# Order edges in a linear attention with a gated feed-forward block: conversions behind kv, gate products behind an x product, projections behind all products

## The chip, the cores and the metric

The kernel runs on one core of one Trainium2 chip. The time of an execution is device microseconds from its start to its end; a profiled execution also has a span, from its first to its last instruction. Times of before are the median of three runs.

## What is computed

Eight batches of 576 tokens pass a linear attention with eight heads of 64, and all 4608 tokens then a gated feed-forward block of width 1536. Everything is float32.

```
q_s = softmax over d of q;  k_s = softmax over s of k
kv  = einsum('bhsd,bhse->bhde', k_s, v)
x   = einsum('bhsd,bhde->bhse', q_s, kv)   # heads side by side: 4608 x 512
out = ((x @ w_a) * (x @ w_b)) @ w_out      # 512 -> 1536 -> 512
```

The host lays the arrays out and passes the weights as raw 64-bit integers; the kernel turns them into float32 itself.

## The kernel before

**Tiles and stages.** Heads go in four pairs g (`NP`), so that one pair fills 128 partitions. Tokens go in nine chunks c of 512 (`NCH`), hidden features in twelve blocks f of 128 (`NF`), taken two at a time (i) from the second chunk on. Products of the attention's result with the weights take each float32 operand as a rounded part and a remainder (`split`, L76: a copy on ACT or DVE, a subtraction on DVE), and sum three matmuls.

**The start (L587 to L623).** For each pair of the first batch the exponential of k is made and transposed (`kv_soft_t`), q's softmax is made, `kv_product` multiplies k with v (PSUM tile pk, den, kv) and `kv_split` makes kvh and kvl, both on DVE. `q_transpose` gives pq and its parts qh (ACT) and ql (DVE); `x_product` multiplies them with kvh and kvl into px, three matmuls, and ACT and DVE split px into an operand tile xo. Behind the second pair stands `convert_f(0)`, behind the fourth `convert_f(1)`.

**Conversions.** `convert_f(f)` turns three raw tiles of block f into weights: two of the gate (`convert_ab`) and one of w_out (`convert_wo`). Each goes through `to_float` (L87): two ACT steps (L99, L100), a DVE shift (L102, raw<-wy), a POOL addition (L103, wr), a DVE merge (L104, wy). `convert_ab` then issues a store of wy on SP (dy), splits it (ACT copy and DVE subtraction, ws) and, for three of four tiles, stores the parts (dw); `convert_wo` stores wy into the w_out tile (wo_w<-wy, L128). The raw tiles share a ring of 11 buffers (tag xo) with the operand tiles of x.

**The first chunk (L633 to L648).** For each f: raw loads of a later block, `convert_f(f + 2)`, one call of `attend()` (the next chunk's attention, a list of ten entries: entry 0 holds the k and v loads of one pair alone, later entries a load, a softmax and a product of different pairs), `gate_first(f)` (24 matmuls into pt, n = 0 and 1; ga copied by ACT at L433 and multiplied by DVE at L434), and `project_first` of the block before (L458, po). At f = 11 the operands of the second chunk are made (`x_operands`), which need the x products of all four pairs (px of c = 1).

**Later chunks (L660 to L725).** Each pair of blocks takes seven products (`product`, L449, 12 matmuls each) in place of eight, with sums between them on DVE (u2, u3, cc) and a split of each gated block (gh on ACT, gl on DVE); `project` (L463) adds a block's 12 matmuls to four output tiles po. The projections of the pair before go between the products, but those of blocks 8 and 9, and of 10 and 11, of the last chunk are left for L724. `store` copies po out of PSUM, in the last chunk by halves (L477 on ACT, L478 on DVE), and issues the store on SP.

**What sets the order.** The framework plans each engine's instruction order ahead, by its own timeline and the order of the program: an instruction ready earlier in the plan goes ahead of one that stands earlier in the program but is ready later. On the chip each engine takes its instructions in the planned order. All DMAs are issued on one queue, SP. `tc.issue_after(ins)` adds an edge from `ins` to each instruction that the block makes on the engine of `ins`, and to no other.

## Time and profile before

| | us |
|---|---|
| median of three runs (lowest, highest) | 990.01 (989.1, 992.04) |
| profiled execution | 986.57 |
| its span | 984.5 |
| PE busy in the span | 948.7 (96%) |
| DVE, ACT, POOL busy | 632.5, 391.7, 112.8 |
| mean granted clock of PE | 0.99 of full speed |

PE is TensorE's matmuls and PEld its weight loads, DVE is VectorE, ACT ScalarE, POOL GpSimd; SPq is the queue that issues the DMAs. A matmul's row gives the time to its modelled end, and matmuls overlap, so that the sum of a group can pass the time to the next row. In a row of the timeline the square brackets tell how long the engine stood before it, and what released it.

### The profile page before, as it was taken

The page shows a single profiled execution, that of the slowest core. Times are in us where ns is not written, and L with a number is a line of the kernel's source. Part 1 is how long each engine was busy: PE and PEld are TensorE (multiplying, and loading weights), DVE is VectorE, ACT ScalarE, POOL GpSimd, SP SyncE. Part 2 cuts the span into 40 slices and gives each one's busy share as a digit, 9 for nine tenths or more (in the row PEclk, how much of TensorE's full clock was granted, in tenths as well). Part 3 has the DMA queues.
Part 4 walks back from the last instruction along what each step waited for, and adds up shares of the span by engine and source line. Part 5 has one row for each costly group of instructions (what it writes and reads, how often), then busy time and mean ns, then how long its engine had stood idle before and what let it go on. Part 6 is the DMA issues. An engine that isn't in the chain of part 4 may idle for free.

```text
span 984.5 us, 16997 instructions
## 1 busy us (share of the span) xinstructions
PE 948.7 (96%) x6171; PEld 854.0 (87%) x6171; DVE 632.5 (64%) x1259; ACT 391.7 (40%) x1087; POOL 112.8 (11%) x96
## 2 busy tenths in 40 slices
PE   3889999999999999999999999999999999999998
PEld 3757666899999999999999999999999999899996
DVE  7797786988686665656566657565656545653443
ACT  8666675542372325322442335223532263221111
POOL 3245344531000000000000000000000000000000
PEclk9799999999999999999999999999999999999999
DMA  9699858999989967997699779977998679767761
GB/s 346 228 412 397 340 207 293 358 332 303 307 279 338 321 241 280 334 334 259 240 339 328 267 258 341 320 264 252 337 295 295 232 282 288 269 230 262 256 212 46
DMA packets 93682, 283.64 MB, mean 288 GB/s; under 512 B 10848, under 2 KB 11424, under 8 KB 93600
## 3 DMA queue, kind: packets, MB, share of 16 engines
q1 hardware_dynamic: 93600, 282.57, 81.9%
q8 instruction: 49, 0.80, 0.3%
q14 instruction: 33, 0.27, 0.1%
HBM read 241.40 MB, written 37.98 MB: 284 GB/s over the span
## 4 chain that ended last, share of the span: by engine, by line
PE 70%; DMA 6%; DVE 2%; ACT 1%; issue 1%; SPq 0%; DVEq 0%
PE po L468 24%; PE kp L449 12%; PE ka L449 12%; PE kx L449 12%; PE ky L449 6%; DMA mr<-dq 4%; DMA qtt<-in_q_late 2%; PE pk L251 2%; PE px L381 2%; DMA dq<-sst 1%; DVE ws L82 0%; ACT qt L323 0%; SPq L347 0%; DVE ql L82 0%; ACT gh L79 0%
## 5 line engine op out<-in xcount | busy, mean ns | idle before, releaser
L468 PE MATMUL po<-wo_w,gh 128*128 128x512 f32 x768 | 226.5, 394 | 1.0 <-ACT gh L79 1.0
L449 PE MATMUL kx<-xo,ws 128*128 128x256 f32 x1152 | 164.8, 284 | 0.0
L449 PE MATMUL ka<-xo,ws 128*128 128x256 f32 x1152 | 163.1, 285 | 0.9 <-DVE cc L720 0.7
L468 PEld LDWEIGHTS po<-wo_w,gh 128*128 128x128 f32 x768 | 138.8, 189 | 27.3 <-ACT gh L79 1.4
L449 PE MATMUL kp<-xo,ws 128*128 128x256 f32 x1152 | 158.3, 284 | 1.1 <-DVE u L693 1.0
L449 PEld LDWEIGHTS ka<-xo,ws 128*128 128x128 f32 x1152 | 152.1, 192 | 4.5 <-DVE cc L720 0.9
L449 PEld LDWEIGHTS kx<-xo,ws 128*128 128x128 f32 x1152 | 151.9, 191 | 3.5 <-issue 0.5
L449 PEld LDWEIGHTS kp<-xo,ws 128*128 128x128 f32 x1152 | 148.2, 191 | 3.9 <-DVE u L693 1.2
L468 PE MATMUL po<-wo_w,gl 128*128 128x512 f32 x384 | 136.9, 395 | 0.0
L79 ACT CAST gh<-cc 128x512 fp32r<-128x512 f32 x96 | 57.6, 620 | 147.4 <-DVE cc L717 144.1
L716 DVE TENSOR_TENSOR cc<-kp,u 128x512 f32<-128x512 f32 x48 | 33.0, 688 | 89.1 <-PE kp L449 88.8
L323 ACT ACTIVATE qt<-qt,st 128x64 f32<-128x64 f32 x224 | 75.0, 336 | 34.7 <-DVE st L320 30.5
L468 PEld LDWEIGHTS po<-wo_w,gl 128*128 128x128 f32 x384 | 71.2, 188 | 15.3
L449 PE MATMUL ky<-xo,ws 128*128 128x256 f32 x576 | 78.5, 285 | 2.5 <-ACT xo L79 2.1
L426 PE MATMUL pt<-xo,ws 128*128 128x512 f32 x288 | 76.1, 415 | 3.0 <-ACT ga L433 3.0
L449 PEld LDWEIGHTS ky<-xo,ws 128*128 128x128 f32 x576 | 72.9, 192 | 3.2 <-ACT xo L79 2.4
L82 DVE TENSOR_TENSOR gl<-cc,gh 128x512 fp32r<-128x512 f32 x96 | 66.9, 704 | 9.6 <-ACT gh L79 9.4
L426 PEld LDWEIGHTS pt<-xo,ws 128*128 128x128 f32 x288 | 55.0, 194 | 19.3 <-ACT ga L433 4.0
L707 ACT COPY cc<-kx 128x256 f32<-128x256 f32 x48 | 17.7, 370 | 130.8 <-PE kx L449 122.1
L706 DVE TENSOR_TENSOR cc<-kp,u 128x512 f32<-128x512 f32 x48 | 32.9, 685 | 54.8 <-PE kp L449 54.8
L219 POOL PARTITION_ALL_REDUCE mx<-m x20 | 14.1, 704 | 467.2 <-DVE m L205 435.4
L355 ACT ACTIVATE qtt<-qtt 128x512 f32<-128x512 f32 x28 | 17.7, 633 | 103.9 <-DVE qtt L354 77.4
(127 smaller groups left out, 1241.8 us busy)
## 6 DMA issues: line engine op xcount, KB each, us to landing
ws<-dw SPq DMA_DIRECT2D x312, 512.0 KB, 5.2
dw<-ws SPq DMA_DIRECT2D x42, 512.0 KB, 5.0
mr<-dq SPq DMA_DIRECT2D x56, 256.0 KB, 6.5
raw<-in_w_ab SPq DMA_DIRECT2D x24, 512.0 KB, 7.9
out<-ot SPq DMA_DIRECT2D x36, 256.0 KB, 4.8
vt<-in_v SPq DMA_DIRECT2D x28, 325.0 KB, 7.3
qt<-in_q SPq DMA_DIRECT2D x32, 256.0 KB, 5.2
kt<-in_k SPq DMA_DIRECT2D x24, 320.0 KB, 5.8
```

Source lines behind the costliest of these rows:

```text
L79: nc.scalar.copy(out=hi, in_=src)
L82: nc.vector.tensor_tensor(out=lo, in0=src, in1=hi.bitcast(F32), op=ALU.subtract)
L251: nc.tensor.matmul(pk, kt[:, j].rearrange("p h d -> p (h d)"), vt[:, j], start=(j == 0), stop=(j == J - 1),)
L323: nc.scalar.activation(out=qt[:, j, h], in_=qt[:, j, h], func=AF.Exp, bias=st[:, h, 0, j:j + 1], accum_out=st[:, h, 1, j:j + 1],)
L355: nc.scalar.activation(out=qt, in_=qt, func=AF.Exp)
L381: nc.tensor.matmul(px[:, s], w, m[:, s], start=(i == 0), stop=(i == 2))
L426: nc.tensor.matmul(pt, w[:, wp], x[g][:, xp], start=(i == 0), stop=(i == 3 * NP - 1))
L449: nc.tensor.matmul(pt[:, n], w[:, n, wp, c], x[:, xp, c], start=(first and n == 0 and i == 0), stop=(i == 5), skip_group_check=True,)
L468: nc.tensor.matmul(po[t], a[:, ts], wo[f][:, w], start=(f == 0 and i == 0), stop=(f == NF - 1 and i == 2),)
L706: nc.vector.tensor_tensor(out=cc[:, 3], in0=kp, in1=u3, op=ALU.add)
L707: nc.scalar.copy(out=cc[:, 0, 0], in_=kx[:, 0])
L716: nc.vector.tensor_tensor(out=cc[:, 1], in0=kp, in1=u2, op=ALU.add)
```

## The change

The products and sums stay as they are. Edges of order are added at four places. The conversions of block 1 are made behind the kv subtractions of pairs 2 and 3; the first call of `attend` stands behind that of pair 3; the gate products of the first chunk's last block stand behind the second chunk's x product of pair 2; the projections that are left at the end stand behind the last product, and those of the last two blocks go one output tile after the other. The last chunk's output tiles are copied whole, the even ones on DVE, the odd ones on ACT.

```diff
@@ -76,10 +76,20 @@
     def split(hi, lo, src, hi_engine="act"):
 
         if hi_engine == "act":
-            nc.scalar.copy(out=hi, in_=src)
+            a = nc.scalar.copy(out=hi, in_=src)
         else:
-            nc.vector.tensor_copy(out=hi, in_=src)
-        nc.vector.tensor_tensor(out=lo, in0=src, in1=hi.bitcast(F32), op=ALU.subtract)
+            a = nc.vector.tensor_copy(out=hi, in_=src)
+        return a, nc.vector.tensor_tensor(out=lo, in0=src, in1=hi.bitcast(F32), op=ALU.subtract)
+
+    @contextmanager
+    def behind(point):
+
+        with ExitStack() as pinned:
+            for ins in marks.get(point, ()):
+                pinned.enter_context(tc.issue_after(ins.ins))
+            yield
+
+    marks = {}
 
 
     wo = {}
@@ -267,7 +277,7 @@
     def kv_split(b, g, kv):
         kvh = sb.tile([P, P], F32R, name=f"kvh{g}")
         kvl = sb.tile([P, P], F32R, name=f"kvl{g}")
-        split(kvh, kvl, kv, "dve")
+        marks["kv", b, g] = split(kvh, kvl, kv, "dve")[1:]
         kvs[b, g] = (kvh, kvl)
 
 
@@ -366,7 +376,7 @@
             )
         qh = sb.tile([P, T], F32R, name="qh", bufs=1)
         ql = sb.tile([P, T], F32R, name="ql", bufs=1)
-        split(qh, ql, pq)
+        marks["q"] = split(qh, ql, pq)
         return qh, ql
 
     def x_product(c, g, qhl, tag="at"):
@@ -378,7 +388,8 @@
         for b, s in ((b0, slice(0, n0)), (b1, slice(n0, T)))[:b1 - b0 + 1]:
             kvh, kvl = kvs[b, g]
             for i, (w, m) in enumerate(((kvh, qh), (kvh, ql), (kvl, qh))):
-                nc.tensor.matmul(px[:, s], w, m[:, s], start=(i == 0), stop=(i == 2))
+                ins = nc.tensor.matmul(px[:, s], w, m[:, s], start=(i == 0), stop=(i == 2))
+        marks["px", c, g] = (ins,)
         return px
 
 
@@ -446,12 +457,13 @@
             i = 0
             for c in range(2):
                 for wp, xp in ((0, 0), (0, 1), (1, 0)):
-                    nc.tensor.matmul(
+                    ins = nc.tensor.matmul(
                         pt[:, n], w[:, n, wp, c], x[:, xp, c],
                         start=(first and n == 0 and i == 0), stop=(i == 5),
                         skip_group_check=True,
                     )
                     i += 1
+        return ins
 
     def project_first(f, g, po):
         for t in range(TT):
@@ -460,22 +472,24 @@
                 start=(f == 0), stop=(f == NF - 1),
             )
 
-    def project(f, ghl, po):
+    def project(f, ghl, po, one_by_one=False):
         gh, gl = ghl
-        for t in range(TT):
-            ts = slice(t * P, (t + 1) * P)
-            for i, (a, w) in enumerate(((gh, 0), (gh, 1), (gl, 0))):
-                nc.tensor.matmul(
-                    po[t], a[:, ts], wo[f][:, w],
-                    start=(f == 0 and i == 0), stop=(f == NF - 1 and i == 2),
-                )
+        with ExitStack() as in_turn:
+            for t in range(TT):
+                ts = slice(t * P, (t + 1) * P)
+                for i, (a, w) in enumerate(((gh, 0), (gh, 1), (gl, 0))):
+                    ins = nc.tensor.matmul(
+                        po[t], a[:, ts], wo[f][:, w],
+                        start=(f == 0 and i == 0), stop=(f == NF - 1 and i == 2),
+                    )
+                if one_by_one:
+                    in_turn.enter_context(tc.issue_after(ins.ins))
 
     def store(c, po):
         for t in range(TT):
             ot = sb.tile([P, DM], F32, name="ot", tag="wr", bufs=4)
-            if c == NCH - 1:
-                nc.scalar.copy(out=ot[:, 0:H], in_=po[t][:, 0:H])
-                nc.vector.tensor_copy(out=ot[:, H:], in_=po[t][:, H:])
+            if c == NCH - 1 and t % 2 == 0:
+                nc.vector.tensor_copy(out=ot, in_=po[t])
             else:
                 nc.scalar.copy(out=ot, in_=po[t])
             nc.sync.dma_start(out=out[c * T + t * P:c * T + (t + 1) * P, :], in_=ot)
@@ -615,12 +629,20 @@
             q_soft_first(qt)
         kv_split(0, g, kv_product(kt, vt, ("po0", "po1")[odd]))
         qhl = q_transpose(qt, ("at", "k1")[odd])
+        marks["q", g] = marks["q"]
         px = x_product(0, g, qhl, ("po2", "po3")[odd])
         x = xo_tile([P, 2, T])
-        split(x[:, 0], x[:, 1], px)
+        marks["x", g] = split(x[:, 0], x[:, 1], px)
         x0.append(x)
-        if odd:
-            convert_f(g // 2)
+        if g == 1:
+            convert_ab(0, 0)
+            convert_ab(0, 1)
+            convert_wo(0)
+    with behind(("kv", 0, 2)):
+        convert_ab(1, 0)
+        convert_ab(1, 1)
+    with behind(("kv", 0, 3)):
+        convert_wo(1)
 
 
     early = (B11, T2, T3, T1)
@@ -636,14 +658,20 @@
                 last_load = load_f(n)
         if f + 2 < NF:
             convert_f(f + 2)
-        if f:
+        if f == 1:
+            with behind(("kv", 0, 3)):
+                attend()
+        elif f:
             attend()
         if f == NF - 1:
             sy[0] = sums(0)
             x_operands(xfs[1], early + late, xo)
-        ghl = gate_first(f, x0)
+        last_f = f == NF - 1
+        with behind(("px", 1, 2) if last_f else None):
+            ghl = gate_first(f, x0)
         if pending is not None:
-            project_first(*pending, po)
+            with behind(("px", 1, None) if last_f else None):
+                project_first(*pending, po)
         pending = (f, ghl)
     pend = [(pending[0], pending[1], 0, po)]
 
@@ -652,7 +680,10 @@
         if not pend:
             return
         f, ghl, c, po = pend.pop(0)
-        (project if c else project_first)(f, ghl, po)
+        if c:
+            project(f, ghl, po, c == NCH - 1 and f >= NF - 2)
+        else:
+            project_first(f, ghl, po)
         if f == NF - 1:
             store(c, po)
 
@@ -716,13 +747,14 @@
             nc.vector.tensor_tensor(out=cc[:, 1], in0=kp, in1=u2, op=ALU.add)
             nc.vector.tensor_tensor(out=cc[:, 1, 0], in0=cc[:, 1, 0], in1=cc[:, 1, 1], op=ALU.mult)
             g1 = g_split(2 * i, cc[:, 0:2, 0])
-            product(ka, operand(A22), x[T4], False)
+            last_product = product(ka, operand(A22), x[T4], False)
             nc.vector.tensor_tensor(out=cc[:, 2], in0=ka, in1=u2, op=ALU.add)
             last = nc.vector.tensor_tensor(out=cc[:, 2, 0], in0=cc[:, 2, 0], in1=cc[:, 2, 1], op=ALU.mult)
             g2 = g_split(2 * i + 1, cc[:, 2:4, 0])
             pend += [(2 * i, g1, c, po), (2 * i + 1, g2, c, po)]
-    while pend:
-        run_pending()
+    with tc.issue_after(last_product.ins):
+        while pend:
+            run_pending()
 
 
 def kernel(**inputs):
```

## Rows read from the trace of the kernel before

**Rows 1.** The page's engines: busy us, share of the span, instructions.

```profile
PE 948.7 (96%) x6171; PEld 854.0 (87%) x6171; DVE 632.5 (64%) x1259; ACT 391.7 (40%) x1087; POOL 112.8 (11%) x96
```

**Rows 2.** Table by stage: stretch, length, busy us of each engine, PEclk, DMA, GB/s.

```profile
25.00:38.10 13.10, 9.42 (x51) 8.16 (x50) 13.10 (x26) 9.94 (x28) 5.07 (x3) 0.76 0.52 201
38.10:50.80 12.70, 11.91 (x53) 9.47 (x53) 6.40 (x22) 8.63 (x29) 3.13 (x3) 0.80 0.74 274
50.80:70.00 19.20, 17.43 (x63) 11.43 (x61) 19.12 (x28) 11.98 (x22) 11.17 (x8) 1.00 1.03 411
...
165.80:170.00 4.20, 1.97 (x12) 1.77 (x13) 3.50 (x6) 3.44 (x7) 0.00 (x0) 0.95 1.03 382
170.00:175.00 5.00, 5.00 (x33) 5.00 (x32) 5.00 (x8) 2.06 (x4) 2.89 (x2) 0.70 1.02 383
...
250.00:955.00 705.00, 701.97 (x4888) 656.03 (x4888) 422.08 (x879) 238.90 (x703) 14.08 (x20) 1.00 0.83 286
```

**Rows 3.** Timeline of DVE, 24 to 47 us: start, us, instruction.

```profile
25.06 0.41 DVE L102 TENSOR_SCALAR raw<-wy 128x512 int32<-128x512 int32 x1
...
26.00 1.76 DVE L82 TENSOR_TENSOR ws<-wy,ws 128x512 fp32r<-128x512 f32 x1
...
28.76 0.16 DVE L256 TENSOR_SCALAR den<-pk 128x1 f32<-128x1 f32 x1
28.84 0.68 DVE L104 SCALAR_TENSOR_TENSOR wy<-wy,wr 128x512 int32<-128x512 int32 x1
...
35.57 1.27 DVE L82 TENSOR_TENSOR ws<-wy,ws 128x512 fp32r<-128x512 f32 x2
...
37.82 0.29 DVE L82 TENSOR_TENSOR kvl<-kv,kvh 128x128 fp32r<-128x128 f32 x1
```

**Rows 4.** Timeline of POOL, 0 to 60 us.

```profile
25.56 1.65 POOL L103 TENSOR_TENSOR wr<-raw,wr 128x512 int32<-128x512 int32 x1 [0.97 <-DVE raw L102]
```

**Rows 5.** Timeline of PE, 36 to 52 us.

```profile
37.84 0.80 PE L381 MATMUL px<-qh,kvh 128*128 128x512 f32 x1
...
50.18 2.10 PE L426 MATMUL pt<-xo,ws 128*128 128x512 f32 x8 [0.79 <-ACT ga L433]
```

**Rows 6.** Timeline of SP, 36 to 50 us.

```profile
37.48 0.48 SPq L128 DMA_DIRECT2D wo_w<-wy  x1
41.74 0.34 SPq L231 DMA_DIRECT2D kt<-in_kt  x1
...
42.59 0.90 SPq L116 DMA_DIRECT2D raw<-in_w_ab  x2
```

**Rows 7.** Timeline of PE, 145 to 170 us.

```profile
149.11 4.21 PE L426 MATMUL pt<-xo,ws 128*128 128x512 f32 x16
153.16 0.19 PE L381 MATMUL px<-qh,kvh 128*128 128x64 f32 x1
...
155.93 3.59 PE L458 MATMUL po<-wo_w,ga 128*128 128x512 f32 x8
...
164.41 0.44 PE L381 MATMUL px<-qh,kvh 128*128 128x64 f32 x1
...
167.82 0.39 PE L449 MATMUL ky<-xo,ws 128*128 128x256 f32 x1 [2.05 <-ACT xo L79]
168.42 0.38 PE L449 MATMUL ka<-xo,ws 128*128 128x256 f32 x1 [0.22 <-ACT xo L79]
```

**Rows 8.** Timeline of DVE, 145 to 170 us.

```profile
147.84 0.69 DVE L82 TENSOR_TENSOR ql<-pq,qh 128x512 fp32r<-128x512 f32 x1 [0.31 <-ACT qh L79]
```

**Rows 9.** Timeline: an earlier chunk's ACT copy, then PE, ACT and DVE at the end.

```profile
162.29 0.58 ACT L480 COPY ot<-po 128x512 f32<-128x512 f32 x1 [0.27 <-PE po L458]
...
974.72 2.12 PE L468 MATMUL po<-wo_w,gh 128*128 128x512 f32 x8 [0.99 <-ACT gh L79]
...
980.59 0.37 ACT L477 COPY ot<-po 128x256 f32<-128x256 f32 x1 [0.33 <-PE po L468]
...
981.00 0.42 DVE L478 COPY ot<-po 128x256 f32<-128x256 f32 x1 [0.28 <-ACT ot L477]
```

**Rows 10.** Waits of PE, grouped: total us, times, longest.

```profile
PE kp L449 <- DVE u L693: 1.0, 1, 1.0
```

More of the change, by code (lines that the diff above doesn't have):

```diff
@@ L1 @@
-from contextlib import ExitStack
+from contextlib import ExitStack, contextmanager
 import concourse.bass as bass
```

## The prediction, made blind

> **What bounds the kernel now.** I read the page's table of engines first: PE is busy for 948.7 of 984.5 us, DVE for 632.5 [rows 1]. Only the 36 us in which PE stands, and the stretches at a low clock, can be won by order. A table by stage says where they are [rows 2]. From 250 to 955 us PE is busy 701.97 of 705 us at clock 1.00: 3 us to win in 72% of the span. From 25 to 38.1 us PE is busy 9.42 of 13.1 us at a granted clock of 0.76 of full speed, and DVE all 13.10 us: DVE bounds. From 38.1 to 50.8 us DVE is busy only 6.40 us and DMA at 0.74: something late holds both. From 50.8 to 70 us DVE (19.12 of 19.2) and DMA (1.03) are full again. So the start loses time in 38.1 to 50.8, and the reader should ask which instruction ends that hole's cause. At the change of chunk, PE is busy 1.97 of the 4.2 us from 165.8, and the next 5 us run at clock 0.70 [rows 2]; at the end one gap of 0.99 us stands ahead of the last 24 products [rows 9].
>
> **DVE's order at the start** [rows 3]. The sum of pair 2's k product is read by the first den at 28.76, but its last step, the kvl subtraction, runs at 37.82: 9.1 us for five short instructions. Between them stand the conversions of weight block f=1: three L102 shifts (0.41 each, one of them, at 25.06, ahead of den), three L104 merges (0.68 each) and two ws subtractions (1.27 together), 4.54 us in all, beside f=0's own work, x operands and early attention. PE's x product of pair 2 starts at 37.84, when kvl lands, and the gate of f=1 only at 50.18 [rows 5]. On SP the k load of the next batch leaves at 41.74 and the raw weights of f=2 right behind it at 42.59 [rows 6]; the k load needs a buffer that the k product behind that x product frees.
>
> **Part 1, conversions of f=1 behind kv.** Nothing is added or removed: `issue_after` orders instructions of one engine, and the marks of kv are DVE's, so eight DVE instructions move (4.54 us) and ACT's six first steps and four SP-issued stores of f=1 stay free, though these stores wait for the moved results; behind them on SP stand the k load and the raw loads. POOL's three additions follow the shifts. With them gone, the five steps from den to kvl can take little more than their own length (den 0.16, kvl 0.29, the others alike), so kvl could end at 30.0 instead of 38.11: 8.1 us at most. The gate of f=1 needs the moved blocks; they fit in the 6.3 us that DVE idles from 38.1 to 50.8 (12.7 minus 6.40), and that cover is gone if kvl comes later than about 40. What is late next is f=2's raw load: if the x product starts at some 32, the k load, which left 3.9 us after that start (41.74 less 37.84), leaves near 36, but the store of f=1's wo, 5 us ahead of the raw loads in SP's queue now, can't leave much before 38, since its merge is now behind kv of pair 3 [rows 6]. So the raw loads come some 4.5 us earlier, the gate of f=1 7 to 8. Bounds: gain 8.1, or nothing, or a loss of 4.54 (rival C). I take 5.0, near the load's 4.5, since f=2's weights are the next thing needed and DVE and DMA are full from there.
>
> A collision changes with it. The ws subtraction at 26.00 took 1.76 us while POOL's addition of f=1 ran from 25.56 for 1.65 us [rows 4]; two of the same kind at 35.57, without POOL, took 1.27 together, 0.64 each [rows 3]. So an addition beside such a subtraction costs 1.1 us. Two of f=0's are hit now (26.00 and one at 29.44 of the same length), 2.2 us ahead of kvl, and these go; I take the collisions as merely moved, at no net cost.
> The Trainium skill, page "SBUF — State Buffer", section "Who interferes with whom", says that a DVE instruction with two SBUF inputs contends with a GpSimd instruction that reads SBUF. By it all three moved additions could each strike a two-input subtraction behind kv, 3.3 us against the 2.2 freed: the start would give 3.9, and the sum below 1.1 us less. The trace agrees on the collision, but doesn't show where the moved additions fall.
>
> **Part 2, the first attention call behind kv of pair 3.** I cost it at nothing: the first of ten entries of that list holds only the k and v loads of one pair. Loads are issued on SP, and the mark is a DVE instruction, so no edge arises. The max reductions and exponentials of later calls stay free to run early.
>
> **Part 3, the gate of f=11 behind the x product of pair 2.** Pair 2's operand is ready at 148.53 (ql, 147.84 plus 0.69) [rows 8], but its x product stands at 153.16, behind 16 of the 24 gate products of 149.11 [rows 7]. Pair 3's transpose uses the same PSUM bank and waits for its copy, so its x product comes at 164.41, and ky waits 2.05 us for the last operands at 167.82 [rows 7]; then comes the stretch at clock 0.70, which costs 1.5 us of its 5 (30% of it). With the gate behind it the x product can start at 149 to 152 (the 8 projection products that now follow the gate at 155.93, 3.59 us, may fill in ahead), 1 to 4 us earlier, and the gate's rest then covers pair 3's chain. Bounds: a gain of 2.05 + 0.22 + 1.5 = 3.8, or a loss of 0.5, if PE has only those 3.59 us of projections between 149.11 and 153.16 (4.05 less 3.59). DVE has only 0.7 us free in 165.8 to 170 [rows 2], so part returns as waits for DVE: I take 2.0. The line that puts the projections of f=10 behind the mark ("px", 1, None) finds no such mark and does nothing.
>
> **Part 4, the last projections behind the last product, and one by one.** 48 matmuls keep their count. Now some of f=8 and f=9 lie between the products, and PE waits 0.99 us for ACT's gh at 974.72 [rows 9]; with more of them behind the last product that gap is covered. Cover lost: the waits between products, of which the dearest in the trace is 1.0 us [rows 10], kp on DVE's u. One by one costs nothing, as po tiles already complete one after the other. Bounds: 0 to 0.99; I take 0.95, as the moved 5 to 18 products are worth more than the gap.
>
> **Part 5, the last stores.** The last tile is copied in halves, ACT 0.37 from 980.59, then DVE until 981.42, 0.83 together [rows 9]; the new order is one ACT copy, which took 0.58 in an earlier chunk [rows 9]: 0.25 gained. DVE's copy of the tile before it, by the 0.69 of its nearest like, the subtraction of the same shape out of PSUM [rows 8], fits into the 0.70 us between tiles. Bounds 0 to 0.25. Parts 4 and 5 give 1.2.
>
> **Sum.** 5.0 + 2.0 + 1.2 = 8.2 us. The profiled execution took 986.57 us (span 984.5 and 2.07 around it), so it would take 978.4. The median shown is 990.01, 3.4 us above that execution, so I forecast 990.01 - 8.2 = 981.8 us. About 0.3%, 3 us, is what a measurement of this kernel tells from no change.
>
> **Rivals.**
> A, the forecast, has the chance 0.50.
> B, the hole stays because f=2 decides: the raw loads hang behind a k load whose release doesn't move, and PE, reaching f=2 early, waits there. For it: SP's queue is in order and DVE and DMA are full from 50.8. Against: the release itself stands behind the x product that moves. The start then gives 1.0, the middle 0.5, the end 1.0: 987.5, chance 0.20. Most of that is within 0.3%.
> C, slower: kvl of pair 2 isn't released by the conversions but by PE and ACT (pq and qh of pairs 1 and 2, at a granted clock of 0.76) or by attention work that slips into the holes, which Part 2 leaves free. Then kvl stays near 38, the 4.54 us of DVE work land behind it, with other late work, in the full stretch from 50.8, and the gate of f=1 and the weights of f=2 come late. It decides from the point where kvl ends after 40. Price 4.54, less 1.2 from the end: 993.3, chance 0.15. The same price could come from a planner that, given a new order, leaves new waits in the 3 us that are now lost in 250 to 955.
> D, everything comes back: 8.1 + 3.8 + 1.2 = 13.1, or 976.9, chance 0.15. It needs DVE's hole to close wholly, and the raw loads to pass the k load.
> That the change doesn't do what it says is partly so (Parts 2 and 3), and lies in B.
>
> **Range and chances.** The likeliest case with its bounds runs from 978 to 986; B reaches to 989, D to 976.9, and with 3 us between executions of one kernel (989.1 to 992.04) I take 974 to 990, which leaves out C and the tails. Faster by over 0.3%: A 0.49, D 0.15, B 0.06, so 0.70. Within 0.3%: B 0.14 and some of A and C, 0.17. Slower: 0.13.
>
> **What would show it.** Part 1 is right if kvl of pair 2 ends near 30 to 32, its x product starts near 32, the gate of f=1 near 43 and the raw loads of f=2 near 38, with DVE's hole small. It is wrong if kvl stays, or if PE shows a new wait for ws ahead of f=1 or f=2. Part 3 is right if ky no longer waits for xo, and the clock stays at 1.00 behind it. Part 4 is right if the last 40 or so matmuls are all po without a gap, and Part 5 if one ACT copy of 0.58 precedes the last store. What would make the whole wrong is a set of new waits from 250 us on, where no instruction is pinned.

## The result, and the profile after

The changed kernel takes 997.88 us (median of 8 runs, 993.95 to 1001.36) against 990.03 for the kernel before on the same chips: a ratio of 1.0075 [1.0049, 1.01]. It is slower by about 8 us, where 981.8 was forecast. Its profiled execution took 998.32 us, with a span of 996.0; that of before took 986.57, with 984.5. The two profiles are thus 11.75 us apart and the medians 7.9: the profiles overstate the loss.

First the table by stage, with the windows of [rows 2]; the columns are those of that group.

```profile
25.00:38.10 13.10, 11.61 (x65) 9.06 (x65) 11.89 (x31) 10.87 (x37) 3.33 (x3) 0.89 0.42 163
38.10:50.80 12.70, 10.31 (x49) 7.93 (x50) 9.45 (x22) 10.35 (x25) 5.54 (x5) 1.00 0.96 313
...
250.00:955.00 705.00, 695.06 (x4824) 649.39 (x4823) 419.41 (x877) 238.54 (x701) 14.63 (x20) 1.00 0.83 282
```

The start does what was forecast of it: PE is busy for 11.61 us of the first window instead of 9.42 and its clock is 0.89 instead of 0.76, and DVE's hole behind it is smaller (9.45 us busy against 6.40). But from 250 to 955 us, where the change pins nothing, PE is busy for 695.06 us instead of 701.97. That is where to look.

A second reading lays the two orders of work side by side: the start of the first kx product of a pair of blocks, in the timeline of PE. The table gives it as a difference from before in us (negative is earlier); the last four columns are experiments told below.

| start of | before | after | e1, end alone | e9, after and ring | e10, end and ring | e18 |
|---|---|---|---|---|---|---|
| end of the first chunk's gate | 156.09 | -2.00 | +0.79 | -2.05 | +1.23 | +0.91 |
| chunk 1, pair 1 | 177.09 | -1.64 | +2.83 | -1.82 | +1.83 | -2.03 |
| chunk 1, pair 2 | 199.29 | +2.98 | +2.06 | +2.74 | +1.25 | -2.13 |
| chunk 2, pair 0 | 270.54 | +0.13 | +1.75 | -0.11 | +0.94 | -4.97 |
| chunk 2, pair 1 | 286.13 | +6.10 | +1.75 | +5.02 | +0.95 | +0.01 |
| chunk 3, pair 0 | 373.39 | +6.84 | +1.73 | +6.85 | -0.57 | +0.87 |
| chunk 6, pair 0 | 678.75 | +13.16 | +4.84 | +5.81 | -1.16 | -0.18 |
| chunk 8, pair 5 | 957.92 | +12.27 | +5.31 | +4.35 | -2.56 | +0.05 |

The changed kernel leads until chunk 1 and then loses 13.9 us (from -1.64 to +12.27) in steps: 4.6 between pairs 1 and 2 of chunk 1, of which 2.9 come back by the end of that chunk, 6.0 at the start of chunk 2, and 6.2 behind. The table by stage of that stretch, from the first to the last of these products, for after and then for before:

```profile
175.45:970.19 794.74, 780.49 (x5396) 728.61 (x5396) 480.23 (x1000) 270.72 (x805) 31.84 (x32) 0.99 0.83 282
```

```profile
177.09:957.92 780.83, 774.35 (x5397) 723.02 (x5396) 483.52 (x1001) 270.01 (x805) 34.15 (x34) 1.00 0.84 289
```

PE stands for 14.25 us of it instead of 6.48, which is 7.8 of the 13.9. In the other 6.1 it is busy longer with the same matmuls, at a mean granted clock of 0.99 instead of 1.00. Not all of that need be the clock: e1 and e10, both at 1.00 in this stretch, are busy for 775.15 and 772.89 us.

One caution is in the column of e1: up to the projections at its end that kernel has the order of before, instruction for instruction, and yet this one execution of it lies up to 5.3 us behind that one of before. A step of a few us in one profile proves little by itself; a step that comes back in several kernels, and the medians, do.

**The start.** DVE's timeline of the changed kernel:

```profile
25.91 0.68 DVE L82 TENSOR_TENSOR ws<-wy,ws 128x512 fp32r<-128x512 f32 x1
...
28.50 0.16 DVE L266 TENSOR_SCALAR den<-pk 128x1 f32<-128x1 f32 x1 [1.18 <-PE pk L261]
...
32.80 0.28 DVE L82 TENSOR_TENSOR kvl<-kv,kvh 128x128 fp32r<-128x128 f32 x1
```

From den to kvl it now takes 4.3 us instead of 9.1 [rows 3], and the two ws subtractions of f=0 that took 1.76 and 1.78 beside POOL take 0.68 each. The moved additions of POOL strike merges instead: the one at 34.91, beside additions from 33.55 to 36.10, takes 1.74 instead of 0.68 [rows 3], and the last one, the w_out merge at 39.19, takes 1.37. SP's and PE's timelines tell how little of this reaches the gate of f=1:

```profile
40.58 0.48 SPq L138 DMA_DIRECT2D wo_w<-wy  x1
41.12 1.08 SPq L126 DMA_DIRECT2D raw<-in_w_ab  x2
```

```profile
33.14 0.50 PE L391 MATMUL px<-qh,kvl 128*128 128x512 f32 x1
...
47.43 1.43 PE L437 MATMUL pt<-xo,ws 128*128 128x512 f32 x5 [1.24 <-ACT ga L444]
```

The x product of pair 2 ends 5.85 us earlier (33.64 for 39.49), the gate of f=1 starts 2.75 earlier (47.43 for 50.18 [rows 5]), and the raw loads of f=2 leave 1.5 earlier (41.12 for 42.59 [rows 6]): the w_out store of f=1, which waits for that last merge, leaves only at 40.58, right ahead of them.

**The end of the first chunk**, PE's timeline:

```profile
146.98 0.30 PE L391 MATMUL px<-qh,kvh 128*128 128x64 f32 x1 [0.19 <-DVE ql L82]
...
148.01 5.17 PE L437 MATMUL pt<-xo,ws 128*128 128x512 f32 x22
...
163.67 0.38 PE L460 MATMUL ky<-xo,ws 128*128 128x256 f32 x1 [0.34 <-ACT xo L79]
...
173.56 2.10 PE L460 MATMUL ka<-xo,ws 128*128 128x256 f32 x12 [2.95 <-issue]
```

The x product stands ahead of the gate, as the edge wants it, and ky starts at 163.67 instead of 167.82 with hardly a wait [rows 7]. Up to here the change has gained 4.2 us. At 173.56 half of it goes: this product started at 175.65 before. "issue" names no releaser, so the reader has to look at what reads the output tile ka before the product may write it: u3, on DVE.

```profile
169.41 3.44 DVE L82 TENSOR_TENSOR ws<-ws_y,ws 128x512 fp32r<-128x512 f32 x2
172.78 0.68 DVE L726 TENSOR_TENSOR u<-ka,u 128x512 f32<-128x512 f32 x1
```

u3 stands behind two ws subtractions, of 1.72 us each while POOL adds from 166.72 to 173.98. The Trainium skill, page "SBUF — State Buffer", section "Who interferes with whom", says that a DVE instruction with two SBUF inputs contends with a GpSimd instruction that reads SBUF; the trace agrees (1.72 for 0.64 to 0.68).

The 4.6 us between pairs 1 and 2 come right behind. POOL's, DVE's and PE's timelines of the changed kernel, then DVE's of before:

```profile
180.35 5.79 POOL L192 TENSOR_TENSOR ws_y<-ws_y 128x512 f32<-128x512 f32 x4 [6.37 <-DVE cc L747]
```

```profile
181.96 1.65 DVE L82 TENSOR_TENSOR gl<-cc,gh 128x512 fp32r<-128x512 f32 x1
183.53 1.29 DVE L224 TENSOR_SCALAR m<-ident,mc 128x128 f32<-128x128 f32 x1
```

```profile
184.88 0.80 PE L226 MATMUL pmx<-m,ones 128*128 128x128 f32 x2 [2.31 <-DVE m L224]
187.68 0.47 PE L220 MATMUL pm<-ident,m 128*128 128x128 f32 x1 [2.01 <-DVE kt L232]
187.81 3.76 PE L481 MATMUL po<-wo_w,gh 128*128 128x512 f32 x8
```

```profile
183.68 0.63 DVE L82 TENSOR_TENSOR gl<-cc,gh 128x512 fp32r<-128x512 f32 x1
184.23 0.27 DVE L214 TENSOR_SCALAR m<-ident,mc 128x128 f32<-128x128 f32 x1
```

POOL's fourth set of sums falls on two DVE rows, gl and m, and PE waits for m (a step of the maximum of the next k). They take 2.0 us longer than before, where that set began at 187.23, behind both. Then eight po matmuls take 3.76 us; at the end of the kernel before the same took 2.12 [rows 9]. The granted clock was down behind PE's stands: its mean is 0.83 from 175.45 to 202.28, part of that at 1.2 instead of 2.4 GHz, and 1.00 before in the same stretch of work. PE stands in it for 4.31 us instead of 2.41 and is busy for 22.52 instead of 19.79, so of the 4.6 us 1.9 are waits and 2.7 slower matmuls.

**The late loads.** The rest is a chain that recurs from chunk 2 on. SP issues the load of mr (rows of dq, which the softmax of the next chunk's q adds); DVE adds it (qtt, L364); ACT takes the exponential and makes qh, DVE ql; PE makes px from them. Two places of it in the changed kernel, from SP's, DVE's and PE's timelines:

```profile
264.41 1.09 SPq L357 DMA_DIRECT2D mr<-dq  x2
...
540.09 1.09 SPq L357 DMA_DIRECT2D mr<-dq  x2
```

```profile
272.73 0.69 DVE L364 TENSOR_TENSOR qtt<-qtt,mr 128x512 f32<-128x512 f32 x1 [2.57 <-DMA mr<-dq]
...
276.17 0.68 DVE L573 TENSOR_TENSOR xf<-px,mr 128x512 f32<-128x512 f32 x1
...
550.41 0.69 DVE L364 TENSOR_TENSOR qtt<-qtt,mr 128x512 f32<-128x512 f32 x1 [5.23 <-DMA mr<-dq]
...
551.62 0.68 DVE L737 TENSOR_TENSOR cc<-kp,u 128x512 f32<-128x512 f32 x1
```

```profile
277.00 0.45 PE L391 MATMUL px<-qh,kvh 128*128 128x128 f32 x1 [3.99 <-ACT gh L79]
...
552.35 0.39 PE L460 MATMUL kp<-xo,ws 128*128 128x256 f32 x1 [1.48 <-DVE cc L737]
```

A load issued at 264.41 lets the add run at 272.73, and PE, whose next row is that x product, stands for 3.99 us. (The trace names gh as the releaser, but the product doesn't read gh. It needs qh, ready at 275.72, and an empty PSUM tile, which DVE's xf gives it at 276.85; xf stands behind the add and five other rows in DVE's queue.) At 540.09 it is 10.3 us from issue to add; there PE waits not at px but for the sum cc that stands behind the add in DVE's queue. Behind the first of these stands the clock is down again for a part of the time: its mean is 0.92 up to the first kx product of the next pair, 1.00 before.

**The end**, PE's and ACT's timelines:

```profile
977.39 1.60 PE L460 MATMUL ka<-xo,ws 128*128 128x256 f32 x12
...
982.32 1.59 PE L460 MATMUL kp<-xo,ws 128*128 128x256 f32 x12
```

```profile
991.99 0.58 ACT L494 COPY ot<-po 128x512 f32<-128x512 f32 x1 [0.81 <-PE po L481]
```

The edge holds the projections behind ka, the last product of the program, but the plan puts kp's product behind ka, so 15 of them still stand between the two. There is no gap any more. From the last pair's first product (970.19) to the end of the span it takes 25.83 us, before 26.55; 25.53 in e1, whose order up to there is that of before.

### The profile page after: what moved, and what is told of

It reads as the page before. It is cut to its first block, busy times and chain, and to the rows that moved or that the text cites. A ratio compares the mean times of both kernels' runs of the same rounds, so it can differ in the third digit from the quotient of the medians.

```text
span 996.0 us, 16984 instructions
## 1 busy us (share of the span) xinstructions
PE 952.5 (96%) x6171; PEld 854.5 (86%) x6171; DVE 628.2 (63%) x1257; ACT 391.4 (39%) x1085; POOL 110.3 (11%) x96
## 4 chain that ended last, share of the span: by engine, by line
PE 70%; DMA 13%; DVE 6%; issue 5%; POOL 3%; ACT 3%; SPq 1%; DVEq 0%; POOLq 0%; ACTq 0%
PE po L481 23%; PE ka L460 12%; PE kp L460 12%; PE kx L460 12%; DMA mr<-dq 7%; PE ky L460 6%; DMA qtt<-in_q_late 3%; POOL wr L113 3%; PE pk L261 2%; PE px L391 2%; DVE wy L114 1%; DMA raw<-in_w_ab 1%; DMA dy<-wy 1%; DMA wo_raw<-in_w_out 1%; PE po L470 1%
## 5 line engine op out<-in xcount | busy, mean ns | idle before, releaser
L481 PE MATMUL po<-wo_w,gh 128*128 128x512 f32 x768 | 231.8, 399 | 0.0
L481 PEld LDWEIGHTS po<-wo_w,gh 128*128 128x128 f32 x768 | 141.1, 192 | 26.5 <-ACT gh L79 0.3
L481 PE MATMUL po<-wo_w,gl 128*128 128x512 f32 x384 | 139.1, 396 | 0.0
L437 PE MATMUL pt<-xo,ws 128*128 128x512 f32 x288 | 74.0, 406 | 5.5 <-ACT ga L444 2.8
```

The source lines that it names most:

```text
L437: nc.tensor.matmul(pt, w[:, wp], x[g][:, xp], start=(i == 0), stop=(i == 3 * NP - 1))
L481: ins = nc.tensor.matmul(po[t], a[:, ts], wo[f][:, w], start=(f == 0 and i == 0), stop=(f == NF - 1 and i == 2),)
```

## Experiments

The ratios are to the kernel before, run on the same chip beside them.

**The parts alone: e1 to e4.** e1 keeps the edges at the end and the stores, e2 the start, e3 the gate's line, e4 start and end.

```diff
 e1 and e4, in the loop over f:
-        with behind(("px", 1, 2) if last_f else None):
+        with behind(None):
             ghl = gate_first(f, x0)
 e2 and e3, at the end (and the stores as before):
-    with tc.issue_after(last_product.ins):
-        while pend:
-            run_pending()
+    while pend:
+        run_pending()
 e1 and e3, at the start:
-        if g == 1:
-            convert_ab(0, 0)
...
+        if odd:
+            convert_f(g // 2)
```

> The kernel before with the edges and stores of the end alone (projections behind the last product and one by one, whole copies). Theory T (the end is a small gain by itself; the changed kernel loses its 11.6 us in 163 to 300 us, 540 to 560 us and 645 to 680 us, where nothing is pinned): order unchanged up to about 950 us, no wait of PE for gh at the end, 0.9 to 1.3 us shorter, ratio 0.998 to 1.000. Rival R1 (the bare run of products at the end waits): ratio over 1.000, with waits of kp or ka behind 970 us.

> The kernel before with the conversions of block 1 behind kv alone. Theory T: the gate of block 1 starts 2 to 3 us earlier as in the changed kernel, but the plan for chunks 1 to 5 changes too; DVE then stands before a qtt addition that waits for its mr load, with sums that PE needs queued behind it, so 3 to 8 us are lost between 170 and 680 us and the sum is 0 to 6 us slower (ratio 1.000 to 1.006). Rival R2 (the gate's edge alone does the harm): 2 to 5 us faster, ratio 0.995 to 0.998, and no lead lost before the end.

> The kernel before with the edge of block 11's gate products behind the x product alone. Theory T: ky no longer waits 2.05 us for its operands, the lead is 1 to 3 us at 170 us, and what is lost again lies before 270 us, since the planned order joins the old one again in chunk 2: ratio 0.997 to 1.002. Rival R2: the 4.6 us that the changed kernel loses between the second and the third pair of blocks of chunk 1 come back in full, and 3 to 6 us are lost in all, ratio 1.003 to 1.006.

> The changed kernel without the gate's edge (conversions behind kv, and the end). Theory T: as the run with the conversions alone, less 1 us. Rival R2: 3 to 6 us faster than before, ratio 0.994 to 0.997. Rival R3 (the parts only harm together): this and each part alone are all faster than before by 1 to 4 us, and only the changed kernel is slower.

| | median, us | ratio |
|---|---|---|
| e1, end | 988.79 | 0.9981 [0.9954, 1.0008] |
| e2, start | 995.44 | 1.006 [1.0037, 1.0083] |
| e3, gate | 996.94 | 1.0079 [1.0052, 1.0106] |
| e4, start and end | 992.79 | 1.0031 [1.0005, 1.0057] |

e1, e2 and e4 came out as their first theory had it; e3 lies above both of its ranges. Of the parts as the change has them, the end is the only one that doesn't lose; e1's interval takes in 1. The start loses although its gate ends 2.25 us earlier (153.84 for 156.09), and e4 is the sum of the two within their intervals. The gate's edge alone loses at once, as PE's timeline of e3 shows:

```profile
148.06 6.17 PE L470 MATMUL po<-wo_w,ga 128*128 128x512 f32 x14
153.67 0.59 PE L391 MATMUL px<-qh,kvh 128*128 128x64 f32 x1
...
155.02 5.20 PE L437 MATMUL pt<-xo,ws 128*128 128x512 f32 x22
...
170.68 0.39 PE L460 MATMUL ky<-xo,ws 128*128 128x256 f32 x1 [2.05 <-ACT xo L79]
```

With the gate held back, 14 projection products of blocks 9 and 10 stand ahead of the x product: 6 that stood ahead of the gate before too (146.94), and the 8 that followed it at 155.93 [rows 7]. The x product starts at 153.67, no earlier than before (153.16). The gate starts 5.9 us later than before and ends 5.0 later, and ky, 2.9 later, has its wait of 2.05 still. In the changed kernel block 10's products stand behind the gate, at 153.93: with the start's edges the plan is another.

The attention call's edge (Part 2) needs no run: without it the planned order of every engine of the changed kernel is the same, instruction for instruction.

**The missing mark: e5.** The gate and block 10's projections both behind the x product; start and end as before.

```diff
-            with behind(("px", 1, None) if last_f else None):
+            with behind(("px", 1, 2) if last_f else None):
                 project_first(*pending, po)
```

> The kernel before with block 11's gate products and also block 10's projections behind the x product of pair 2 (in the changed kernel the projections' edge names a mark that doesn't exist). Theory T2 (with the gate's edge alone the 8 projection products slip ahead of the x product, which then starts at 153.7 us as before, and the whole gate comes behind it, 5 us late; the edge is right, the filler is wrong): the x product starts near 149.5 us, the last gate product ends by 157 us, the wait of ky for xo falls from 2.05 to under 1 us, and the time is 0.996 to 1.002 of before. Rival R2 (gate products behind that x product do harm whatever fills in): ratio 1.004 or more, with the lead lost between 155 and 185 us.

Measured: 990.0 us, 1.0006 [0.9978, 1.0034]. PE's timeline:

```profile
149.46 0.59 PE L391 MATMUL px<-qh,kvh 128*128 128x64 f32 x1
...
165.91 0.38 PE L460 MATMUL ky<-xo,ws 128*128 128x256 f32 x1
```

The x product is 4.2 us earlier than in e3, and ky waits for nothing. The theory held. So the slipped projections were e3's harm, and the line with a mark that is never set was needed for the gate's edge. e5 leads by 4.49 us at the start of chunk 2, and is 0.80 behind one pair later: the lead goes where the changed kernel loses 6.0. PE stands there for 3.3 us at the same x product as the changed kernel. This is a pattern: after, e5, e9, e11, e12 and e18, whose gate's edge moves the x product ahead, all lose 5.0 to 6.5 us between the first two pairs of chunk 2, with that stand at 3.1 to 4.5; e1 to e4, e7, e8, e10 and e17 lose 0.1 at most.

**The add away from DVE: e6 to e8.** If the harm were only that other DVE work queues behind the add that waits for mr, POOL could take the add. e6 is the changed kernel with this edit, e7 the start alone, e8 the end alone.

```diff
-        nc.vector.tensor_tensor(out=qt, in0=qt, in1=mr[:, 0], op=ALU.add)
+        nc.gpsimd.tensor_tensor(out=qt, in0=qt, in1=mr[:, 0], op=ALU.add)
```

> The changed kernel with the addition that waits for mr (qtt<-qtt,mr) made by POOL instead of DVE, all else alike. Theory T: DVE no longer stands before mr loads with sums queued behind it, so of the 12 us lost between the start of chunk 2 and the last pair of blocks 8 or more come back: ratio 0.996 to 1.002. Rival R4 (the loss behind 270 us comes from late loads of weights, from ACT, or from the new PE order): no more than 3 us come back, ratio 1.005 or more.

> The conversions' edges alone, with that addition on POOL. Theory T: the lead of 1.5 to 2.5 us of the start is kept to the end, ratio 0.994 to 0.999 (1.006 without the move to POOL). Rival R4: ratio 1.003 or more.

> The end's edges alone, with that addition on POOL. Theory T: in the order of before PE loses 3 to 7 us behind 250 us to the same waits, and most of that comes back: ratio 0.992 to 0.997 (0.998 without the move). Rival R5 (POOL's two-input additions slow DVE's two-input subtractions by up to 1.1 us each and PE waits for those): ratio 0.999 or more.

Measured: 1.0168 [1.0142, 1.0193], 1.0131 [1.0084, 1.0178] and 1.0043 [1.0015, 1.0071], each slower than the same kernel with the add on DVE, and in the range of a rival. The table of waits on PE from 240 to 960 us, its leading lines (us in total, times, longest) in the changed kernel, e6 and e8:

```profile
PE px L391 <- ACT gh L79: 4.0, 1, 4.0
PE px L391 <- ACT qh L79: 3.3, 3, 1.7
```

```profile
PE px L391 <- ACT qh L79: 6.9, 8, 1.4
PE po L481 <- ACT gh L79: 4.2, 2, 3.7
```

```profile
PE px L391 <- ACT qh L79: 7.9, 6, 3.2
```

With DVE free of the add, PE waits at the x products themselves: in e8 for 7.9 us, where e1 has 4.5, in e6 for 7.3, little less than the 8.5 of the changed kernel, and for 4.2 at projections besides. That theory falls, with a reservation: the add takes 1.32 us on POOL (mean in e8) and 0.69 on DVE (e1), so qh also comes later, and the runs don't separate the two. Rival R5 is borne out in single rows alone: from 300 to 960 us gl's median is 0.68 in both, and the longest of 78 in e8 took 1.03. What is common to all these kernels is that PE has an x product as its next row before the load it hangs on has come through.

**Earlier loads: e9 to e12.** mr has two buffers, so a load can't leave until the second pair before it is done. The ring of eight buffers that held converted weights at the start is idle from chunk 2 on; mr there, as two tiles, is four pairs deep. e9 is the changed kernel with it, e10 the end alone, e11 the changed kernel with e5's line and without the ring, e12 the same with it.

```diff
+        if c >= 3:
+            mr = [sb.tile([P, T], F32, name=f"mr{w}", tag="wy", bufs=8) for w in range(2)]
+            for w in range(2):
+                for h in range(2):
+                    nc.sync.dma_start(
+                        out=mr[w][h * D:(h + 1) * D],
+                        in_=dq[g, h, w * T:(w + 1) * T].unsqueeze(0).broadcast_to([D, T]),
+                    )
+            return qt, mr
```

> Edit: the changed kernel, and from chunk 3 on the two rows of dq go into two tiles of the ring of eight that the weights' raw loads used at the start, so four pairs of loads fit where two did, and each can leave up to two pairs earlier. Theory (the lost time is PE standing at an x product that the replanned order puts ahead of a qh or ql whose dq load comes late): with the loads early, the losses behind chunk 3 (+7.50 to +13.17 us in the changed kernel's profile) go, what was lost up to there stays; ratio at most 1.004, and the rows in which PE waits on an x product for ACT's qh or DVE's ql behind 400 us fall to under half. Rival (the loads only look late, the lost time is another resource or the order of PE itself): ratio 1.005 to 1.010, as the changed kernel's own 1.0075.

> Edit: the end of the change alone, with the same ring for dq. Theory: the kernel of before loses 3 us between 250 and 955 us to its own late loads, of which some 2 lie behind chunk 3; with the end's 1 us, ratio 0.995 to 0.998. Rival: as the end alone, 0.998, or above it by the cost of twice as many dq transfers on SP (4 instead of 2 for each pair).

> Edit: the changed kernel, but with the products of block 10 with wo behind the x product of pair 2 too, as the line of the change with a mark that is never set would have had it. Theory: the gate ends some 3 to 6 us earlier than in the kernel of before, as the two parts alone gave 2.2 and 4.2; the lead is lost again behind it wherever an x product is ahead of its operand, ratio 0.997 to 1.003. Rival (the early gain is simply kept, and the loss of the changed kernel came from the slipped projections): ratio 0.992 to 0.996.

> Edit: the kernel with both the gate and block 10's products behind the x product of pair 2, and the ring for dq from chunk 3 on. Theory: what is lost behind chunk 3 is kept, ratio 0.990 to 0.997, and 2 us or more below the same kernel without the ring. Rival: the same as that kernel without the ring, within 2 us.

| | without the ring | with it, from chunk 3 on |
|---|---|---|
| the changed kernel | 1.0075 [1.0049, 1.01] | e9: 0.9992 [0.9967, 1.0017] |
| end alone | e1: 0.9981 [0.9954, 1.0008] | e10: 0.9914 [0.9886, 0.9942] |
| changed, and e5's line | e11: 1.0024 [0.9995, 1.0054] | e12: 0.9989 [0.9963, 1.0015] |

The ring takes 0.8% from the changed kernel, all that it had lost against before, and 0.7% from the end alone, intervals apart both times; e10, at 982.58 us, beats both kernels. For e11 and e12 the intervals overlap. The mechanism is in the waits of DVE from 300 to 960 us, first of before, then of the changed kernel, then of e9:

```profile
DVE qtt L354 <- DMA mr<-dq: 34.4, 17, 5.1
```

```profile
DVE qtt L364 <- DMA mr<-dq: 36.1, 15, 5.2
```

```profile
DVE qtt L374 <- DMA mr<-dq: 7.6, 6, 2.0
```

The loads are as late in the kernel before. What differs is what reaches PE: there 1.9 us at x products and nothing else. The waits of PE in the changed kernel and e9, in the same stretch:

```profile
PE px L391 <- ACT qh L79: 3.3, 3, 1.7
PE kp L460 <- DVE cc L737: 1.5, 1, 1.5
PE px L391 <- DVE ql L82: 1.2, 3, 0.7
```

```profile
PE px L401 <- ACT qh L79: 1.6, 1, 1.6
```

In the table by pairs, from chunk 2's pair 1 to the end, the changed kernel loses 6.2 us more and e9 gains 0.7. What e9 keeps of the loss, 4.6 in chunk 1 and 5.1 at the start of chunk 2, lies ahead of the ring. One reservation: the ring changes the planned order too, from chunk 2 on, so it is not the loads' time alone that differs. The rows of waits speak for the loads: from 300 to 960 us PE waits at x products for 0 to 1.8 us in all in the kernels with the ring (e9, e10, e12 to e18), and for 1.9 (before) to 7.2 (e2) in before, after, e1 to e5 and e11. The Trainium skill, page "Perfetto Trace Analysis", section "Optimization Strategy", says that a gap repeating on the engine that should be saturated can mean too little room for the next tile, the number of buffers for one. PE's gaps are scattered here rather than repeating, but the two ratios agree with that reading. The theory held for e9 and fell short for e10, which gained more than it said; e11's ratio is where its theory had it, though its gate ends 2.1 us earlier and not 3 to 6; e12 is 5.6 us below e11, as expected, but its 0.9989 is outside the 0.990 to 0.997.

**The ring a chunk earlier: e13 to e16**, `c >= 2` in the same line; e13 the changed kernel, e14 with e5's line, e15 start and end, e16 e5's edges and the end.

> Edit: the changed kernel with the ring for dq from chunk 2 on (e9 had it from chunk 3 on). Theory: in e9 the add at the start of chunk 2 still waited 1.94 us for a load issued at 264.17, and PE 3.1 us at an x product; with the loads early, of the 5 us that e9 lost there 3 or more go: ratio 0.993 to 0.997. Rival (that loss belongs to the order of chunk 1 and 2, not to the loads): ratio 0.998 to 1.001, PE's wait at the x product stays.

> Edit: the kernel with gate and block 10's products behind the x product of pair 2, and the ring for dq from chunk 2 on (e12 had it from chunk 3 on). Theory: e12 lost 6.5 us at the start of chunk 2 and 5 us between pairs 3 and 5 of chunk 2 with waits of PE at x products; both go, ratio 0.987 to 0.994. Rival: as e12, 0.997 to 1.001.

> Edit: the conversions behind kv and the end, without the gate's mark, and the ring for dq from chunk 2 on. Theory: the start's gain of 2.2 us at the gate is kept to the end, so 2 us below the end alone with the ring (0.9914): ratio 0.987 to 0.991. Rival (an early gain never reaches the end, whatever the loads): 0.991 to 0.997.

> Edit: the gate and block 10's products behind the x product of pair 2 and the end, without the conversions behind kv, and the ring for dq from chunk 2 on. Theory: the lead of 2 to 4.5 us that e5 had until the start of chunk 2 is kept to the end: ratio 0.986 to 0.990. Rival (an early gain never reaches the end): 0.991 to 0.997.

Measured: 1.0111 [1.0066, 1.0155], 1.0105 [1.0056, 1.0154], 1.0115 [1.0085, 1.0145] and 1.0083 [1.0047, 1.0119]: all slower and outside every range given, by a cost of the edit itself. SP's timeline of e13:

```profile
228.58 8.32 SPq L359 DMA_DIRECT2D mr<-dq  x12
236.94 1.06 SPq L184 DMA_DIRECT2D ws_y<-dy  x2
```

In chunk 1 the ring isn't idle: the sums of weights (ws_y) use it. The loads of three pairs' mr stand ahead of those of the sums, and leave only at 228.58, behind the store of dq at 226.74 that they read. So the sums' loads leave from 236.94 on, in the changed kernel by 216.50, and POOL's last two sets of sums start at 252.08 and 268.84, there at 210.09 and 220.84. Chunk 1 ends some 20 us late (+21.98 at chunk 2's first product). So these four can't tell what the loss at the start of chunk 2 is. They do show again that nothing is lost behind: e13 goes from +23.12 at chunk 2's pair 1 to +19.05 at the last.

**Each early edge with the ring from chunk 3: e17 and e18.** e17 is start and end, e18 e5's edges and the end.

> Edit: as e15 (conversions behind kv, and the end), but with the ring for dq from chunk 3 on. Theory: the ring from chunk 2 on took the sums' buffers at the end of chunk 1, and that alone made e13 to e16 slow; from chunk 3 on nothing is lost behind 300 us, and what the kernel without the ring (e4) had lost by the start of chunk 2, some 2 us for a gain of 2 at the gate, decides: ratio 0.991 to 0.996, above the end alone with the ring (0.9914) or equal to it. Rival (the early gain of 2 us is kept once the loads are early): 0.987 to 0.990.

> Edit: as e16 (gate and block 10's products behind the x product, and the end), but with the ring for dq from chunk 3 on. Theory: e5 led by 4.5 us at the start of chunk 2 and lost 5.3 us there with a load of dq that the ring from chunk 3 on doesn't reach; nothing is lost behind: ratio 0.989 to 0.994. Rival (the lead is kept): 0.985 to 0.988.

Measured: 985.33 us, 0.9942 [0.9917, 0.9967], and 982.59 us, 0.992 [0.9892, 0.9948]. Both lie where the theory put them, and neither is below the end alone with the ring (0.9914 [0.9886, 0.9942]), so no early gain is seen to arrive; one of 1 or 2 us would be hidden by the intervals. e17 also repeats the ring's effect: it is 0.9% below e4, the same kernel without the ring (1.0031 [1.0005, 1.0057]). For e18 the table by pairs shows where it goes: from -4.97 to +0.01 at the start of chunk 2, with mr still in its two buffers there. For e17 it goes in chunk 1; the table of PE's waits from 156 to 204 us:

```profile
PE kx L470 <- DVE xo L82: 2.4, 1, 2.4
PE ky L470 <- ACT xo L79: 2.1, 1, 2.1
```

Having ended the gate 1.71 us earlier, PE waits for the last x operands as long as before, and 2.4 us at the next product. The start's lead is kept up to pair 1 of chunk 1 only with the gate's edge (-1.64 in the changed kernel, +0.77 in e2), and both together bring the loss of 4.6 us in chunk 1: the seven kernels that have both (after, e6, e9, e11 to e14) lose 4.4 to 4.9 there between pairs 1 and 2, while those with one of them or none don't (e2 and e3 -1.5, e5 +0.1, e18 -0.1). The rows show why: in the seven, POOL's fourth set of sums begins between 179.50 and 180.78 and gl ahead of m takes 1.64 to 1.66 us; in the other thirteen it begins at 185.55 or later, behind both rows, and gl takes 0.63 or 0.64. Why the plan with both edges lets that set run there, and puts the ws subtractions ahead of u3, isn't settled.

## Why the prediction was wrong

**What failed is the step from the stages to the sum.** "From 250 to 955 us PE is busy 701.97 of 705 us at clock 1.00: 3 us to win" was read as a stretch that would stay, so that 8.2 us gained at its two ends would arrive. But the order there is planned anew from what comes before, and 3 us was what that one order lost; this one loses 9.9 (705 less 695.06). With mr in two buffers, whether a load is late for the row in which PE needs it is decided by an order that the change doesn't pin. The sum had no term for new waits, nor for the clock that falls behind them: of the 13.9 us from chunk 1 on, 7.8 are PE standing, and in 6.1 it is busy longer, in part at the lower clock. Rival C named this in its last sentence ("a planner that, given a new order, leaves new waits in the 3 us that are now lost"), at 4.54 us and as a part of 0.15. The last sentence of what would show it wrong, new waits from 250 us on, came true. A second term was put at nothing, "I take the collisions as merely moved, at no net cost": at the start that about held (2.2 us freed, 1.7 taken by two merges), but in chunk 1 the new plan brings POOL's sums onto gl and m, which no sum of the prediction looked at.

**Part 1**, gain 5.0: right in sign, oversized. kvl ends at 33.08 instead of 38.11, so 5.0 of the 8.1 us closed. The gate of f=1 gained 2.75 and the first chunk's end 2.0, since the raw loads of f=2 went only 1.5 earlier, behind the w_out store that the edge itself held until 40.58; the text saw that store in the way, but put it at 38. Two readings of rows were off, without weight: the second shift of f=1, at 28.41, also ran ahead of den, so that 3.7 and not 4.1 us of the moved work lay between den and kvl; and the x product at 37.84 starts with kvh, which kvl follows.

**Part 2**, nothing: right, by the planned order.

**Part 3**, gain 2.0, bounds +3.8 and -0.5: in the changed kernel half right, ky's wait of 2.05 falls to 0.34 and the clock from 150 to 175 us is 0.99 instead of 0.93. But the clock doesn't stay at 1.00 behind it, as the text's own sign wants: the fall comes a few us later and costs more, 0.93 from 175 to 250 us where it was 1.00. Alone (e3), the step that failed is the lower bound: the 8 projection products did fill in ahead, and the x product came 0.5 us later, as that bound had it; but it stopped there, and the gate now stands behind, ends 5.0 us later, and ky with its old wait 2.9 later. That the line with the unset mark does nothing was seen; that, by e5, it was the half that the edge needed was not.

**Parts 4 and 5**, gain 1.2: 0.7 in the changed kernel, 1.0 in e1, whose ratio of 0.9981 takes in 1 with its interval. The gap closed, and the last copy is one of 0.58, as forecast.

So by ky, at 163.67 us, 4.2 of the 7.0 us forecast for Parts 1 and 3 were there, and 0.7 came at the end. Between them the profiled execution lost 16.4: 2.5 up to pair 1 of chunk 1, and 13.9 behind. By e9, the 6.2 behind the start of chunk 2 go when the dq loads come early (with the reservation on the order); the 4.6 in chunk 1 come with both early edges together, by POOL's collisions and the clock; the 6.0 at the start of chunk 2 come with the gate's edge, and by the rows hang on a load of the same kind (the add waits, xf behind it, then PE), but e13 to e16 can't show that, so it is read, not shown.

## What to carry to other kernels

When a planner writes the order, an edge is no local edit: compare the whole planned order, and count a stretch as safe only if it has slack against its loads, not because it lost little in one execution. Where a waiting load feeds the next product, make the load earlier (more buffers) before moving work around it: that gave 0.7% here under an unchanged order up to chunk 2, and the early edges of order gave nothing that the intervals show, with it or without. Price a stand of the busiest engine with the matmuls behind it, too: in one place here 1.9 us of waits cost 4.6, since the clock fell. And an edge that holds work back must name what may fill the place, or something later will.

## What the runs showed that was not expected

Two executions of the same order, before and e1, lie up to 5.3 us apart at the same product: a single profile can't carry a claim of a few us in this kernel.

The load of mr in 256 KB pieces takes 7.2 us (median from issue to landing) in the changed kernel, 6.5 before; in pieces of 128 KB, which the ring needs, 4.2 in e9 and 3.8 in e10, for twice as many. So the ring makes the loads both earlier and shorter, and its effect isn't split between the two.
